# First samples of a speech joint kernel loaded in two halves, with its first products by halves of the channels

## The chip, the cores and the metric

The kernel runs on one core of a Trainium2 chip, alone. A core has TensorE (PE in the profile; its weight loads are listed as PEld), VectorE (DVE), ScalarE (ACT), GpSimd (POOL) and SyncE (SP), which here issues nearly all transfers between the chip's DRAM and the core's memory SBUF. TensorE writes its products into PSUM, eight banks of 512 columns of fp32; VectorE and ScalarE take them from there. The metric is the device time of one execution in microseconds, and the time of a kernel is the median of its runs.

## The reference

Two convolutions of five taps with a stride of two, a projection, and an outer sum over eight label positions with a tanh and a last product. `gelu` is the tanh approximation.

```python
B, T, D, K, U = 2, 4000, 512, 5, 8
h = gelu(sum(xp[:, i:i+T, :] @ w1[i] for i in range(K)))[:, ::2, :]
f = gelu(sum(hp[:, i:i+T1, :] @ w2[i] for i in range(K)))[:, ::2, :]
fe, ge = f @ w_f, g @ w_g
j = tanh(fe[:, :, None, :] + ge[:, None, :, :])
return j @ w_o            # (2, 1000, 8, 512), bf16
```

`xp` and `hp` are padded by two zeros on both sides. The taps of the first convolution are called tap 0 to tap 4 below.

## The kernel before

All operations are first collected as a list (`Plan.op`, `Plan.dma`) with what they read and write; the list's index is the operation's number. `ORDER` then holds, written out as steps from one number to the next, the order in which each engine runs them; SP's queue of transfers is one of these orders. `Plan.edges` finds the dependences, `Plan.emit` puts a semaphore wait ahead of each operation that needs one, and `AFTER` adds a few waits by hand. The costs that operations carry (`cost`, `rate`, `slack`) belong to a model that orders the closing waits; they don't change an instruction. An engine runs its queue strictly in order, so an operation that waits holds up all behind it.

Most of both convolutions is done with a transform: for three outputs at once, sums and differences of samples (`row`, `xa`, `xp`) are multiplied with sums and differences of weights (`w1_t`, `w1_x`), which VectorE and ScalarE make from the taps (`w1part`, helpers at L442, L604 and L605). Until these weights exist, the first 378 outputs of the first sequence are made directly from the taps (`direct`, L762). That is the head of the kernel, and the change is there:

- `load_xr(0)` (L494) brings 512 samples, four consecutive rows to a partition, into `xr[0]` with one transfer of 512 KB; `load_xr(1)` brings 256 more after the first has landed. The taps follow in the order 0, 4, 2, 1, 3 (`TAPS`), 512 KB each, with the transposing loads of `xa` (`load_a`) between them. A few of these issues wait for an earlier landing (`came`).
- Eight warming products of 512 columns on constants (`NWARM`, L550) keep TensorE at work until the samples are there.
- `turn(pp, cost)` (L563) transposes the samples with products against a unit matrix, so that channels lie on the partitions: pp 0 for even output columns (taps 0, 2, 4), pp 1 for odd ones (taps 1, 3). It is called once for each. A call takes both pairs of rows of all four channel blocks; pp 0 is evicted to `eo` in three pieces (one of 512 columns by VectorE, two of 256 by ScalarE), pp 1 in one piece of 1024 by ScalarE. `turn_more` (L585) does the same for `xr[1]`, with two evictions.
- `direct(i, lo, hi)` runs, for each of four blocks of outputs m, four products (the four channel blocks k) of tap i on the columns lo to hi, and adds them up in PSUM bank m. Taps 0, 4 and 2 run first on 254 columns (`NH`), those that the first 512 samples feed, with `turn_more` before tap 2; then these three taps run on the other 124 columns; taps 1 and 3 run on all 378.

After the last tap ScalarE applies gelu from the four banks, and TensorE goes on with the transformed products: first "t2" of the object `xa`, which needs the difference that the step "t2" of `Triple.step` makes in `xa` on VectorE, and the weights `w1_x[1]`.

Much later, `ge` (L807) computes `g @ w_g` and copies its 64 columns to `geT` on ScalarE in `NG` = 24 pieces. From about the middle on (`Seven`, L1063) the last product is computed in groups of seven products for eight, with sums `ss` made by GpSimd or VectorE, evictions `sn` and `og`, and stores to DRAM.

Of the kernel before, what the change touches and what calls it, by code (L numbers as in the profile page):

```python
# [61 lines left out]
        4 1 1 25 4 25 1 1 4 25 4 25 1 1 4 25 4 25 1 1 4 25 4 23 1 1 4 23 4 19 1 1 7 3 3 5 5""",  # L62
}
AFTER = """
    779:726 780:748 854:893 1059:1031 1178:1120 1272:1211 1273:1304 1364:1397 1456:1426 1486:1517 1603:1577"""


class View:
# [1234 lines left out]
```

## Time and profile before

| | us |
|---|---|
| median of 3 runs | 249.22 |
| lowest, highest | 248.97, 250.26 |
| the profiled execution | 248.89 |
| its span, first to last instruction | 247.6 |

The span is what the profile sees; the execution took 1.3 us more. A row of the timeline gives start, length, engine, line, operation, output<-input and count, and in brackets the idle time ahead of it with what ended it. A row of groups gives count, busy time, mean nanoseconds of one, and the idle time ahead. A row of the windows gives a stretch, its length, then busy time with count for PE, PEld, DVE, ACT and POOL, then the granted clock, the share of the DMA engines and GB/s. SPq is SP issuing a transfer, not the transfer.

### The profile page before, as it was taken

To read this page: it belongs to the slowest core of one execution; us is meant where nothing else is said; L and a number is where in the kernel's file an instruction comes from. 1 tells how busy PE (TensorE), PEld (TensorE's weight loads), DVE (VectorE), ACT (ScalarE), POOL (GpSimd) and SP (SyncE) were. 2 spreads that over 40 slices of the span, in tenths; PEclk is the share of its full clock that TensorE was granted. 3 is DMA by queue.
4 is the path that set the end of the run, shared out by engine and by line. 5 is a ranking of instruction groups with operands and counts; after the bars stand their busy time and mean duration, and the time that the engine had idled before them with its cause. 6 is when DMAs were issued, how large, how long until landed. Compare 5 with 4: busy or idle time off the path is not lost.

```text
span 247.6 us, 5295 instructions
## 1 busy us (share of the span) xinstructions
PE 244.1 (99%) x1966; PEld 184.5 (75%) x1968; DVE 212.4 (86%) x391; ACT 196.7 (79%) x355; POOL 88.0 (36%) x97
## 2 busy tenths in 40 slices
PE   8999999999999999999999999999999999999995
PEld 4969976666666666666456888777888888888884
DVE  1799996967999994795959988889999998899984
ACT  4897848458786475645599999799999999999863
POOL 1000000000000000000003988958988677658770
PEclk9999999999999999999999999999999999999999
DMA  7999999989000061000001044232543464653468
GB/s 236 303 217 186 158 189 182 195 183 345 6 3 0 0 213 45 0 3 1 0 3 42 10 134 143 76 111 85 173 129 101 156 192 149 226 180 106 161 217 283
DMA packets 54839, 31.83 MB, mean 129 GB/s; under 512 B 31870, under 2 KB 54558, under 8 KB 54814
## 3 DMA queue, kind: packets, MB, share of 16 engines
q1 hardware_dynamic: 54526, 31.34, 47.5%
q8 instruction: 15, 0.25, 0.5%
q10 hardware_dynamic: 288, 0.16, 0.2%
q14 instruction: 10, 0.08, 0.1%
HBM read 7.60 MB, written 16.38 MB: 97 GB/s over the span
## 4 chain that ended last, share of the span: by engine, by line
PE 98%; ACT 0%; issue 0%
PE acc L455 98%; PE acc L571 0%; ACT jT L447 0%; PE acc L592 0%; ACT ost L447 0%
## 5 line engine op out<-in xcount | busy, mean ns | idle before, releaser
L447 ACT ACTIVATE jT<-feT,geT 128x1000 bf16<-128x1000 f32 (+4 forms) x72 | 73.3, 1067 | 1.6 <-POOL ss L1085 1.3
L442 DVE TENSOR_TENSOR og<-acc,sn 128x512 bf16<-128x512 f32 x90 | 58.0, 684 | 2.5 <-PE acc L455 1.3
L1085 POOL TENSOR_TENSOR ss<-jT 128x512 f16<-128x512 bf16 x38 | 43.7, 1159 | 39.8 <-ACT jT L447 35.0
L455 PE MATMUL acc<-tw,ss 128*128 128x256 f16 x360 | 50.3, 273 | 0.0
L455 PE MATMUL acc<-row,jT 128*128 128x334 bf16 (+2 forms) x288 | 49.9, 296 | 0.0
L455 PE MATMUL acc<-wo_sb,jT 128*128 128x256 bf16 (+3 forms) x266 | 40.7, 277 | 0.1
L455 PEld LDWEIGHTS acc<-tw,ss 128*128 128x128 f16 x360 | 34.3, 98 | 6.8 <-ACT sn L556 1.0
L455 PEld LDWEIGHTS acc<-row,jT 128*128 128x128 bf16 x288 | 27.2, 97 | 11.3 <-DVE acc L598 0.7
L556 ACT ACTIVATE sn<-acc 128x512 f32<-128x512 f32 x55 | 32.4, 624 | 3.3 <-PE acc L455 3.2
L455 PEld LDWEIGHTS acc<-wo_sb,jT 128*128 128x128 bf16 x268 | 25.9, 98 | 5.7
L447 ACT ACTIVATE hT<-acc 128x334 bf16<-128x334 f32 (+3 forms) x36 | 15.2, 431 | 16.3 <-PE acc L455 16.2
L447 ACT ACTIVATE sd<-acc 128x334 f32<-128x334 f32 (+2 forms) x48 | 20.4, 434 | 8.9 <-PE acc L455 7.7
L557 DVE COPY sn<-acc 128x512 f32<-128x512 f32 x35 | 23.6, 686 | 3.3 <-PE acc L455 3.1
L455 PE MATMUL acc<-xp,jT 128*128 128x334 bf16 (+1 forms) x144 | 26.4, 305 | 0.0
L1085 POOL TENSOR_TENSOR ss<-ss,jT 128x512 f16<-128x512 f16 x19 | 22.0, 1159 | 9.9 <-DVE ss L1085 7.6
L1085 POOL TENSOR_TENSOR ss<-jT,ss 128x512 f16<-128x512 bf16 x19 | 22.0, 1160 | 6.8 <-DVE ss L1085 6.6
L439 POOL MEMSET hT<- 128x8 bf16 (+2 forms) x6 | 0.8, 148 | 56.0 <-ACT hT L447 43.7
L442 DVE TENSOR_TENSOR row<-row 128x1336 bf16<-128x1336 bf16 (+2 forms) x24 | 19.2, 813 | 0.0
L455 PEld LDWEIGHTS acc<-xp,jT 128*128 128x128 bf16 x144 | 14.0, 97 | 6.4
L455 PE MATMUL acc<-wo_sb,ss 128*128 128x256 bf16 x120 | 18.5, 273 | 0.0
L598 DVE SCALAR_TENSOR_TENSOR acc<-acc,sd 128x334 f32<-128x334 f32 (+2 forms) x24 | 11.8, 494 | 7.6 <-PE acc L455 7.4
L455 PE MATMUL acc<-tw,jT 128*128 128x256 f16 x120 | 18.0, 273 | 0.0
(113 smaller groups left out, 395.0 us busy)
## 6 DMA issues: line engine op xcount, KB each, us to landing
out_dram<-og SPq DMA_DIRECT2D x44, 256.0 KB
jT<-in_w_dram SPq DMA_DIRECT2D x10, 512.0 KB, 6.0
out_dram<-og SPq DMA_DIRECT2D x16, 128.0 KB, 2.0
xr<-in_x_dram SPq DMA_DIRECT2D x1, 512.0 KB, 3.4
wf_sb<-in_w_f_dram SPq DMA_DIRECT2D x1, 512.0 KB, 3.8
wg_sb<-in_w_g_dram SPq DMA_DIRECT2D x1, 512.0 KB, 4.8
wo_sb<-in_w_o_dram SPq DMA_DIRECT2D x1, 512.0 KB, 7.0
out_dram<-ost SPq DMA_DIRECT2D x4, 128.0 KB, 1.9
```

What stands on the lines that cost most here:

```text
L439: pl.op("pool", lambda e: e.memset(v.ap, 0.0), (), (v,))
L442: pl.op(eng, lambda e: e.tensor_tensor(out=o.ap, in0=a.ap, in1=b.ap, op=op), (a, b), (o,), 0.02 + 2.14e-3 * o.ap.free_size() if eng == "po ...
L447: pl.op("act", lambda e: e.activation(o.ap, i.ap, func, scale=scale, bias=0.0 if bias is None else bias.ap), rd, (o,), o.ap.free_size() * ...
L455: ins = e.matmul(o.ap, lhsT=l.ap, rhs=r.ap, start=start and n == 0, stop=stop and n == len(pairs) - 1, skip_group_check=not check)
L556: pl.flex({"act": (lambda e: e.activation(o.ap, v.ap, ACT.Copy), 0.05 + n * 0.833e-3), "dve": (lambda e: e.tensor_copy(out=o.ap, in_=v.ap) ...
L557: "dve": (lambda e: e.tensor_copy(out=o.ap, in_=v.ap), 0.065 + n * 1.04e-3)}, (v,), (o,))
L598: pl.op(eng, lambda e: e.scalar_tensor_tensor(out=o.ap, in0=a.ap, scalar=f, in1=b.ap, op0=ALU.mult, op1=add), (a, b), (o,), vec_cost(o, (a ...
L1085: fn = lambda e, o=S[i], x=x, y=y, op=op: e.tensor_tensor(out=o.ap, in0=x.ap, in1=y.ap, op=op)
```

## The change

In the head:

- `xr[0]` comes in two transfers of 256 KB, `load_x2(0)` with the first two rows of each partition and `load_x2(1)` with the other two. The second samples (`load_xr(1)`) wait for the second of these.
- Taps 0 and 4 come in two transfers each, channel blocks 0 and 1, then 2 and 3 (`load_w1h`). The queue is: samples, samples, tap 0, tap 0, first half of tap 4, second samples, second half of tap 4, tap 2, and then as before.
- The transposes of the first rows (both pp) are two operations that wait for the first half of the samples alone; those of the second rows follow by channel block for pp 0 and in two pieces for pp 1. Each channel block of pp 0 lies in a PSUM bank of its own (`KB`) and is evicted by itself: blocks 0 and 1 by VectorE, 2 and 3 by ScalarE, 256 columns each.
- `direct` takes a slice of channel blocks. Tap 0 and tap 4 run on 254 columns in two halves of the channels each, with `turn_more` between the halves of tap 4; then both on the other 124 columns; tap 2 runs once, on 378 columns.
- Six warming products in place of eight.

Elsewhere: `NG` is 28; the modelled rate and size of the stores are other numbers. The orders of all engines are written anew. In the head, both evictions of `turn_more` go to ScalarE; VectorE gives up two scalings of `w_x` and one of `row` and gets four scalings of 512 columns; one difference of `xp` (index 220 before) comes later on VectorE. Up to about 185 us the order of TensorE is otherwise the same but for a few exchanges; behind it the orders of TensorE, VectorE and ScalarE differ in many places, with the same operations. Some entries of `AFTER` are others.

```diff
-    NWARM = 8
+    NWARM = 6
...
-    NG = 24
+    NG = 28
...
-        came = [load_xr(0)]
+        def load_x2(half):
+            dst = xr[0][2 * half:2 * half + 2].map(lambda a: a.rearrange("p r k c -> p r (k c)"))
+            src = x[0, 0:4 * P, :].rearrange("(p r) c -> p r c", r=4)[:, 2 * half:2 * half + 2]
+            return pl.dma("sp", lambda e: e.dma_start(dst.ap, src), (), (dst,), nbytes=2 * P * 1024, rate=370e3, slack=0.1 * half)
+
+        load_x2(0)
+        came = [load_x2(1)]
...
-        came.append(load_w1(TAPS[0]))
-        came.append(load_w1(TAPS[1]))
-        came.append(load_xr(1, came[0]))
+        def load_w1h(i, *ks):
+            for k in ks:
+                v, src = w1_sb[i, k:k + 2], w1[i].rearrange("(k c) d -> c k d", c=P)[:, k:k + 2]
+                o = pl.dma("sp", lambda e, v=v, src=src: e.dma_start(v.ap, src), (), (v,), nbytes=262144, slack=(0.5 if i == TAPS[1] else 0.2) if k else 0.2)
+            return o
+
+        came.append(load_w1h(TAPS[0], 0, 2))
+        load_w1h(TAPS[1], 0)
+        load_xr(1, came[0])
+        came.append(load_w1h(TAPS[1], 2))
         came.append(load_w1(TAPS[2], came[0]))
         load_a(4, 0, after=came[1])
-        came.append(load_w1(TAPS[3], came[-3]))
+        came.append(load_w1(TAPS[3], came[-2]))
         load_a(2)
-        came.append(load_w1(TAPS[4], came[-3]))
+        came.append(load_w1(TAPS[4], came[-2]))
         load_a(1, 3, 5)
...
+        KB = (4, 1, 5, 6)
+
+        def turned(pp, k):
+            if pp:
+                at_k = psb[:, 7 * 1024:8 * 1024].rearrange("p (k r c) -> p r k c", r=2, k=NK)[:, :, k]
+                return View(at_k, np.array([7]), True)
+            at_k = psb[:, KB[k] * 1024:KB[k] * 1024 + 2 * P].rearrange("p (r c) -> p r c", r=2)
+            return View(at_k, np.array([KB[k]]), True)
+
+        def turn(pp, r, ks, cost):
+            v = [turned(pp, k) for k in ks]
+
+            def fn(e):
+                for k, pv in zip(ks, v):
+                    ins = e.transpose(pv.ap[:, r], xr[0].h[:, 2 * r + pp, k, :], ident.h[:, :])
+                return ins
+            pl.op("pe", fn, (xr[0][2 * r + pp], ident[:]), tuple(v), cost * len(ks))
+
+        def turn_out(pp, k=None):
+            if pp:
+                v = View(psb[:, 7 * 1024:8 * 1024].rearrange("p (k r c) -> p k c r", r=2, k=NK), np.array([7]), True)
+                o = eo[1, :, 16:16 + 2 * P].map(lambda a: a.rearrange("p k (c r) -> p k c r", r=2))
+                act(o, v, ACT.Copy)
+                return
+            o = eo[0, k, 16:16 + 2 * P].map(lambda a: a.rearrange("p (c r) -> p c r", r=2))
+            v = turned(0, k).map(lambda a: a.rearrange("p r c -> p c r"))
+            if k < 2:
+                pl.op("dve", lambda e, o=o, v=v: e.tensor_copy(out=o.ap, in_=v.ap), (v,), (o,), vec_cost(o, (v,)))
+            else:
+                act(o, v, ACT.Copy)
...
-        def direct(i, lo=0, hi=ND):
+        def direct(i, lo=0, hi=ND, ks=slice(0, NK)):
             for m in range(NK):
                 mm(ps.cols(m * NT + lo, hi - lo),
-                   [(w1_sb[i, k, m * P:(m + 1) * P], eo[i % 2, k, 15 + i // 2 + lo:15 + i // 2 + hi]) for k in range(NK)],
-                   i == TAPS[0] and lo == 0, i == TAPS[-1], False)
+                   [(w1_sb[i, k, m * P:(m + 1) * P], eo[i % 2, k, 15 + i // 2 + lo:15 + i // 2 + hi]) for k in range(NK)[ks]],
+                   i == TAPS[0] and lo == 0 and ks.start == 0, i == TAPS[-1], False)
...
-        turn(0, 0.215)
-        direct(TAPS[0], 0, NH)
-        turn(1, 0.215)
-        direct(TAPS[1], 0, NH)
-        turn_more(0.46)
-        direct(TAPS[2], 0, NH)
-        for i in TAPS[:3]:
+        turn(0, 0, range(NK), 0.095)
+        turn(1, 0, range(NK), 0.095)
+        for k in range(NK):
+            turn(0, 1, (k,), 0.095)
+            turn_out(0, k)
+        for k in range(0, NK, 2):
+            turn(1, 1, range(k, k + 2), 0.095)
+        turn_out(1)
+        for i in TAPS[:2]:
+            for k in range(0, NK, 2):
+                direct(i, 0, NH, slice(k, k + 2))
+                if i and not k:
+                    turn_more(0.46)
+        for i in TAPS[:2]:
             direct(i, NH, ND)
+        direct(TAPS[2])
         for i in TAPS[3:]:
             direct(i)
```

The first numbers of the orders of VectorE and of SP, the rest of which is as long as the kernel's list (SP: 6 and 7 the samples, 9 and 10 tap 0, 11 and 13 tap 4, 12 the second samples, 14 tap 2):

```diff
     "dve": """
-        0 46 50 1 2 -4 3 3 3 -41 44 13 -12 1 33 -26 9 -8 27 -1 -32 7 16 -29 -3 34 9 -18 26 -6 -25 -9 8 27 -36 18 20 -1 2
+        0 49 2 55 6 -7 3 -1 13 9 -11 9 -8 6 26 -47 9 3 36 -9 -2 -31 1 23 2 -22 40 -17 8 -23 8 -9 35 -17 18 1 2 -1 2 3
...
     "sp": """
-        6 2 1 1 1 1 1 1 1 1 1 1 1 2 2 1 1 1 1 2 1 1 1 1 1 248 1 1 1 1 1 1 2 1 1 1 1 1 254 1 1 168 3 33 33 4 1 1 30 4 33
+        6 1 2 1 1 1 1 1 1 1 1 1 1 1 1 1 2 2 1 1 1 1 2 1 1 1 1 1 254 1 1 1 1 1 1 2 1 1 1 1 1 254 1 1 172 3 33 33 4 1 1 30
```

More of the change, by code (lines that the diff above doesn't have):

```diff
@@ L561, in evict @@
                 pl.op("dve", lambda e: e.tensor_copy(out=o.ap, in_=v.ap), (v,), (o,), vec_cost(o, (v,)))
-        def turn(pp, cost):
-            for bk, k0, k1 in (((4, 0, 2), (5, 2, 3), (6, 3, 4)), ((7, 0, 2), (7, 2, 4)))[pp]:
-                at_k = psb[:, bk * 1024:(bk + 1) * 1024].rearrange("p (k r c) -> p r k c", r=2, k=NK)[:, :, k0:k1]
-                pv = View(at_k, np.array([bk]), True)
-                def fn(e, pv=pv, k0=k0, k1=k1):
-                    for k in range(k0, k1):
-                        for r in range(2):
-                            ins = e.transpose(pv.ap[:, r, k - k0, :], xr[0].h[:, 2 * r + pp, k, :], ident.h[:, :])
-                    return ins
-                pl.op("pe", fn, (xr[0][:], ident[:]), (pv,), cost * (k1 - k0))
-                if pp:
-                    if k0 == 0:
-                        continue
-                    k0, pv = 0, View(psb[:, bk * 1024:(bk + 1) * 1024].rearrange("p (k r c) -> p r k c", r=2, k=NK), pv.cells, True)
-                o = eo[pp, k0:k1, 16:16 + 2 * P].map(lambda a: a.rearrange("p k (c r) -> p k c r", r=2))
-                v = pv.map(lambda a: a.rearrange("p r k c -> p k c r"))
-                if k0 or pp:
-                    act(o, v, ACT.Copy)
-                else:
-                    pl.op("dve", lambda e, o=o, v=v: e.tensor_copy(out=o.ap, in_=v.ap), (v,), (o,), vec_cost(o, (v,)))
@@ L1020, in store2 @@
             dst = out[b, t:t + 2 * P, u, :].rearrange("(t p) d -> p t d", p=P)
-            pl.dma("sp", lambda e: e.dma_start(dst, s.ap), (s,), (), sem_of(key), 4 * P * P * 4)
+            pl.dma("sp", lambda e: e.dma_start(dst, s.ap), (s,), (), sem_of(key), 4 * P * P * 4, 350e3)
         def store(jt, src, key, eng="sp", cl=slice(0, NT)):
@@ L1030, in store @@
                 dst = out[b, t:t + n, u, cl]
-                pl.dma(eng, lambda e, s=s, dst=dst: e.dma_start(dst, s.ap), (s,), (), sem_of(key), 2 * n * P * 4)
+                pl.dma(eng, lambda e, s=s, dst=dst: e.dma_start(dst, s.ap), (s,), (), sem_of(key), 2 * n * (cl.stop - cl.start), 350e3)
                 lo += n
```

16 lines of the change are left out of this document (8 added, 8 removed), and 59 rows, old and new, of the table ORDER.

## The prediction

> **What bounds the kernel now.** I read the page first (busy shares), then the chain that ended last, then the first 20 us as a timeline.
>
> ```profile
> span 247.6 us, 5295 instructions
> PE 244.1 (99%) x1966; PEld 184.5 (75%) x1968; DVE 212.4 (86%) x391; ACT 196.7 (79%) x355; POOL 88.0 (36%) x97
> ...
> 0.77 3.57 PE acc L455 x8
> ...
> 5.04 0.67 ACT jT L447 x2
> ...
> 5.79 3.66 PE acc L455 x32
> 9.45 0.45 PE acc L592 x8
> 9.90 120.64 PE acc L455 x928
> ```
>
> TensorE is the bound: the chain stays on it from 9.90 us to the end. A change of the head can only pay by letting products start earlier, and each microsecond must then survive 235 us of stages whose other queues are nearly full. What holds the head:
>
> ```profile
> 0.74 0.39 SPq L482 DMA_DIRECT2D xr<-in_x_dram  x1
> 1.19 0.97 SPq L473 DMA_DIRECT2D jT<-in_w_dram  x2
> 4.15 0.34 SPq L482 DMA_DIRECT2D xr<-in_x_dram  x1
> 4.17 1.31 PEld L571 LDWEIGHTS acc<-ident,xr 128*128 128x128 bf16 x16 [0.73 <-DMA xr<-in_x_dram]
> 4.83 0.69 DVE L583 COPY jT<-acc 128x512 bf16<-128x512 bf16 x1 [3.70 <-PE acc L571]
> 5.04 1.69 ACT L447 ACTIVATE jT<-acc 128x256 bf16<-128x256 bf16 x3 [2.81 <-PE acc L571]
> 5.76 3.41 PEld L455 LDWEIGHTS acc<-jT 128*128 128x128 bf16 x32 [0.28 <-ACT jT L447]
> 7.50 0.43 DVE L442 TENSOR_TENSOR hw<-jT 128x512 f16<-128x512 bf16 x1 [1.98 <-DMA jT<-in_w_dram]
> 16.79 0.27 PEld L455 LDWEIGHTS acc<-jT 128*128 128x128 bf16 x3 [0.29 <-DMA jT<-in_w_dram]
> ```
>
> The samples land at 4.15, the transposes run from 4.18, the evictions to SBUF end at 5.7, the first product starts at 5.79. The last two rows matter as much: VectorE starts its weight sums only when the whole of tap 4 is there (7.50), and at 16.79 the last tap's products already wait for their weights.
>
> **The first product.** Prices of TensorE come from the groups by form of the first 20 us, those of DMA from the issues (size, time to landing):
>
> ```profile
> L455 PE MATMUL acc<-const-bfloat16-1.0 128*128 128x512 bf16 x8 | 3.6, 628 | 0.8 <-PEq L1288 0.8
> L571 PE MATMUL acc<-ident,xr 128*128 128x128 bf16 x16 | 1.5, 268 | 0.0
> L455 PE MATMUL acc<-jT 128*128 128x254 bf16 x48 | 5.6, 272 | 0.1
> L455 PE MATMUL acc<-jT 128*128 128x124 bf16 x48 | 2.8, 217 | 0.0
> L455 PE MATMUL acc<-jT 128*128 128x378 bf16 x32 | 5.4, 323 | 0.0
> ...
> xr<-in_x_dram SPq DMA_DIRECT2D x1, 512.0 KB, 3.4
> out_dram<-ost SPq DMA_DIRECT2D x4, 128.0 KB, 1.9
> xr<-in_x_dram SPq DMA_DIRECT2D x1, 256.0 KB, 4.0
> ```
>
> A half load of the samples (256 KB) is not in the trace with an empty queue. Its bounds are 1.9 us (128 KB) and 3.4 us (512 KB); on the line between them it takes 2.4, so it lands between 2.6 and 4.15. I take 3.4, nearer the larger load, because that one is also the first of the kernel. The second half lands when the whole load did, 4.15 to 4.25. Six warming products end at 0.77 + 6 x 0.45 = 3.4, so the removed two cost nothing there. The eight transposes of the first half (0.1 each at the early, slow pace) run 3.45 to 4.3. From 4.3 the four of the even rows follow, one for each channel block; each is evicted by itself. The eviction of 512 columns took 0.69 on VectorE; 256 columns are half of that, 0.35, two in sequence: from 4.66 (the copy began 0.65 after the first transpose now, 0.35 after one alone) to 5.37. With the 0.09 of issue, the first product starts at 5.45 instead of 5.79: a gain of **0.34**, between 0 (the second half lands late, or VectorE's two copies cost 0.5 each) and 0.45 (transposes at 4.18). Its two blocks of tap 0 are there: the whole of tap 0 had landed before 5.79.
>
> **The products behind it.** Their number on 254 columns stays at 32 for taps 0 and 4; by halves of channels the same instructions come in another order. Tap 2 becomes 16 products of 378 columns (5.4 / 32 x 16 = 2.70) instead of 16 of 254 (1.87) and 16 of 124 (0.93): 0.1 less by busy sums, which hold the overlap at each group's end; I take 0.02 and keep 0 to 0.1. The eight transposes L592 move between the halves of tap 4. Tap 4's second half is now issued behind the wait for the second samples and behind the later samples (xr, 256 KB). That is the place in the stream where these landed: 4.15 + 4.0 = 8.15. TensorE reaches it at 5.45 + 24 x 0.109 + 0.45 = 8.5 (step 3.66 / 32 less the drain). No stall, 0.35 to spare. SP now has five issues instead of three ahead of its first wait (about 0.45 each, to 3.1, below 4.2), and behind it three instead of two; the transposing load after them waited until 5.56 for tap 0 anyway, so the order behind is late by nothing. The uncovered price would be 0.45.
>
> **The last tap.** TensorE would reach it 0.36 earlier, at 16.4, but it waited for the weights until 16.79. That load was issued at 10.54:
>
> ```profile
> jT<-in_w_dram SPq DMA_DIRECT2D x1, 512.0 KB, 6.2
> ...
> 15.40:16.40 1.00, 1.00 (x8) 0.58 (x6) 1.00 (x4) 0.94 (x2) 0.00 (x0) 1.00 0.28 29
> ...
> q8 instruction: 1, 0.02, 5.8%
> ```
>
> The last two columns of the second row are DMA share and GB/s: from 15.4 to 16.4 us almost nothing moves, as when one engine is behind the others. The third row is from 13.2 to 14.4: a fetch of instructions went through one engine there. I take it for TensorE's code, which would be fetched as TensorE proceeds through it (not shown by this row); 18 pairs of instructions fewer come before it then, so it moves to about 14.2, when most of the tap is through. I estimate the landing at 16.4, between 15.5 (fetch out of the way) and 16.75 (as now). So of 0.36 some 0.35 would pass here, or only the present stall if nothing changes.
>
> **VectorE's queue.** This is what caps the gain:
>
> ```profile
> 7.50:37.20 29.70, 29.70 (x301) 25.20 (x300) 29.26 (x67) 23.26 (x50) 0.77 (x6) 1.00 1.10 203
> ...
> L557 DVE COPY jT<-acc 128x512 bf16<-128x512 bf16 x1 | 0.4, 426 | 0.0
> L605 DVE TENSOR_SCALAR row<-xa 128x832 bf16<-128x832 bf16 x2 | 0.8, 376 | 0.0
> L605 DVE TENSOR_SCALAR w_x<-hw 128x512 bf16<-128x512 f16 x2 | 0.6, 291 | 0.0
> ...
> 18.37 0.59 DVE L442 TENSOR_TENSOR xa<-xa 128x824 bf16<-128x824 bf16 x1
> 19.37 0.25 PE L455 MATMUL acc<-xa,w_x 128*128 128x206 bf16 x1
> ```
>
> VectorE (fourth pair of figures) is busy 29.26 of 29.70 us from the landing of tap 4 on. With tap 4 whole only at 8.15 it starts 0.65 later. The order text takes from it one eviction (0.43), two scalings of w_x (0.29 each) and one of row (0.38), and gives it four scalings of 512 columns (0.29 each, nearest row): 0.23 less. About 0.2 more were waits for ScalarE near 10 us, which vanish. So the difference that the first product on xa needs ends at 18.96 + 0.65 - 0.43 = 19.18 instead of 18.96, and that product starts at 19.2 instead of 19.37. ScalarE takes 1.4 us more but has 6.4 us free in that window (29.70 - 23.26).
>
> The sum of the head: 0.36 earlier, cut to **0.2** by VectorE; 0 to 0.4 with the bounds above.
>
> **The rest.** Four more copies of geT (24 to 28) cost ScalarE 0.07 each, 0.28, by the first row below; ScalarE waits 2.41 behind them (second row), which hides it, and uncovered it costs 0.28. From about 185 us on the order of all engines is another one; the work is the same. What it can win is what TensorE waits for there:
>
> ```profile
> 115.26 1.55 ACT L447 ACTIVATE geT<-acc 128x3 f32<-128x3 f32 x22
> 119.70 0.45 ACT L447 ACTIVATE fT<-acc 128x334 bf16<-128x334 f32 x1 [2.41 <-PE acc L455]
> ...
> PEld acc L455 <- ACT sn L556: 1.3, 7, 0.3
> PEld acc L455 <- DVE og L442: 0.4, 2, 0.3
> ```
>
> These are load-side waits of 1.7 us in all; part is hidden under running products. A reshuffle may win or lose about 0.4 of it. I take 0.
>
> The profiled execution took 248.89 us (span 247.6 and 1.3 around it); the sum gives 248.7 for its like. The median of the runs, 249.22, is 0.33 above that execution, so I predict 249.0.
>
> **The clock.** By the first group above a warming product costs 3.6 / 8 = 0.45 us for 512 columns, 0.88 ns a column; 378 columns later take 0.45 ns a column. The fast pace begins among the transposes:
>
> ```profile
> 4.18:4.99 0.81, 0.81 (x8) 0.81 (x9) 1.00 1.06 374
> 5.11:5.60 0.49, 0.49 (x9) 0.38 (x7) 1.00 1.02 324
> ```
>
> Eight in 0.81 us, then nine in 0.49: the pace doubles near 5.1, 4.3 us after the first product. If it doubles there again, nothing is lost. The Trainium skill ("TensorE: Matmul & The Clock Gate", Part 1) says that the clock opens after a busy window of about 3.4 us that runs freely; the trace's 4.3 us does not contradict it. The same page's Part 4 says that transposes don't count as busy; by that rule this change, which puts transposes and a gap of 0.3 us where two warming products were, could miss the window. No run here shows which.
>
> **Rivals.**
> (a) *The clock opens one window later* (slower). Of the 3.4 us before 5.1 now 2.5 are products; with six warming products 1.7. If that decides, the pace doubles at 5.1 + 3.4 = 8.5, and products from 5.45 to 8.5 run at half pace: 3.05 / 2 = 1.5 us lost, less the 0.36 gained: 1.1 slower, **250.3**. For it: fewer products before the turn. Against: the transposes keep the array busy, and the pace turned while they ran. Decides from a start of fast products after 6 us on.
> (b) *VectorE's later start comes through* (slower). If the moved work doesn't shrink its queue, 0.65 late less 0.41 (the time between 18.96 and 19.37) is 0.25, and the later reader at 30.80 us sees up to 0.4 of it: **249.6**. For: the 29.26 of 29.70. Against: 0.43 of relief counted above.
> (c) *All of the head and a better tail*: 0.36 + 0.4: **248.45**. For: the last tap may land at 15.5, ahead of its readers. Against: VectorE.
> (d) *The split does not split*: both halves land near 4.15, the first transposes start there, and the even rows' only at 5.0; the first product is at 6.1, 0.3 late: **249.5**. Against: the loads stand in one queue in order; the Trainium skill ("DMA: Bandwidth & Descriptors", Queues, rings and completion order) has each DMA engine take its descriptors in ring order, which no run here shows yet.
>
> **Chances.** Forecast 0.50, (a) 0.12, (b) 0.18, (c) 0.15, (d) 0.05. The forecast's own range is 248.6 to 249.4, the sum's 0 to 0.4 and 0.2 for the median of few runs. A difference under 0.5% (1.25 us: 247.97 to 250.47) cannot be told from no change by a measurement of this kernel, whose three runs spread from 248.97 to 250.26. A third of (c) goes below it: 0.05. Of (a) half goes above, and a little of (b) and (d): 0.09. The rest, 0.86, is no change. The range, 248.2 to 250.2, reaches over (b), (d), most of (c) and to the edge of (a).
>
> **What would show it.** First transpose near 3.45, first product near 5.45, VectorE's first sum near 8.2, the last tap's first product before 16.6 without a wait, the first product on xa at 19.2. The forecast is wrong if the pace doubles after 6 us, if that last product is not before 19.37, or if TensorE's waits after 185 us differ by more than 0.4.

## The result and the profile after

| | before | after |
|---|---|---|
| median of 11 runs each | 249.19 (248.73 to 250.26) | 250.44 (249.87 to 250.73) |
| the profiled execution | 248.89 | 250.59 |
| its span | 247.6 | 249.2 |
| first product on xa | 19.37 | 21.42 |

The ratio is 1.0049, with a 95% interval of 1.0037 to 1.0061: slower by half a per cent, 1.25 us. The loss is in the head: the first product on xa is 2.05 us late, and the execution ends 1.70 late. First the page of the changed kernel, its span, its busy line and the chain that ended last by engine:

```profile
span 249.2 us, 5278 instructions
...
PE 245.1 (98%) x1948; PEld 184.9 (74%) x1950; DVE 211.3 (85%) x390; ACT 197.6 (79%) x361; POOL 87.9 (35%) x97
...
PE 97%; DMA 2%; DVE 0%; issue 0%; SPq 0%; ACT 0%
```

TensorE is still the bound, and it is busy 1.0 us more than before with 18 recorded products fewer (two warming ones, and 16 by tap 2 in one piece). Its timeline in the head shows where:

```profile
3.39 1.03 PE L591 MATMUL acc<-ident,xr 128*128 128x128 bf16 x8
5.09 1.03 PE L591 MATMUL acc<-ident,xr 128*128 128x128 bf16 x8 [0.66 <-DMA xr<-in_x_dram]
6.22 4.37 PE L456 MATMUL acc<-jT 128*128 128x254 bf16 x24
10.43 0.61 PE L615 MATMUL acc<-ident,xr 128*128 128x128 bf16 x8
10.88 10.52 PE L456 MATMUL acc<-jT 128*128 128x254 bf16 x88
21.42 0.80 PE L456 MATMUL acc<-xa,w_x 128*128 128x206 bf16 x7
```

The first transposes start at 3.39 as forecast. The second ones wait for the second half of the samples until 5.09, the first product runs at 6.22 and not at 5.45, and 24 products take 4.37 us where 32 took 3.66 before. The windows tell why: in two microseconds of products on 254 columns TensorE (first pair of figures) does 10 in the changed kernel and did 19 in the kernel before.

```profile
6.30:8.30 2.00, 2.00 (x10) 1.40 (x11) 0.00 (x0) 0.90 (x1) 0.00 (x0) 1.00 0.96 286
```

```profile
5.85:7.85 2.00, 2.00 (x19) 1.72 (x20) 0.35 (x2) 1.23 (x2) 0.00 (x0) 1.00 1.07 369
```

The clock column says 1.00 in both, so the pace has to be read from the products. By their starts in the trace, the step halves to 0.109 us at 9.5 in this execution; before, it did so among the transposes at 5.1. From 10.88 to xa TensorE shows no wait (gaps under 0.15 us are not listed); VectorE's difference, which the first product on xa needs too, ends at 21.36 (shown under VectorE further down).

Second, the loads. SP's timeline after:

```profile
0.74 0.87 SPq L498 DMA_DIRECT2D xr<-in_x_dram  x2
1.65 1.46 SPq L521 DMA_DIRECT2D jT<-in_w_dram  x3
5.06 0.34 SPq L483 DMA_DIRECT2D xr<-in_x_dram  x1
5.44 0.45 SPq L521 DMA_DIRECT2D jT<-in_w_dram  x1
5.93 0.47 SPq L474 DMA_DIRECT2D jT<-in_w_dram  x1
6.50 3.77 SPq L493 DMA_TRANSPOSE xa<-in_x_dram  x2
10.32 0.58 SPq L474 DMA_DIRECT2D jT<-in_w_dram  x1
```

The same rows before, from tap 2 on:

```profile
4.53 0.44 SPq L473 DMA_DIRECT2D jT<-in_w_dram  x1
5.56 3.03 SPq L492 DMA_TRANSPOSE xa<-in_x_dram  x2
8.64 0.58 SPq L473 DMA_DIRECT2D jT<-in_w_dram  x1
```

Tap 2 is issued 1.40 late (5.93), the transposing loads 0.94 (6.50), tap 1 1.68 (10.32). Completions, from the semaphore records of the traces ("again" is a second trace of the changed kernel, e18 below; us from the start of the span):

```
                      before   after   again
samples, last part      4.13    5.04    4.71
tap 0, last part        5.55    6.49    6.17
tap 4, last part        7.47    8.58    8.61
tap 2                   9.57   11.07   10.60
tap 1                  13.24   14.59   16.13
tap 3                  16.75   18.14   18.39
```

The windows of 2 us, first before, then after (the last two columns are the DMA share and GB/s):

```profile
2.00:4.00 2.00, 2.00 (x6) 0.61 (x4) 0.00 (x0) 0.22 (x2) 0.00 (x0) 1.00 0.91 322
...
6.00:8.00 2.00, 2.00 (x21) 1.71 (x19) 0.51 (x2) 1.23 (x2) 0.00 (x0) 1.00 1.07 368
```

```profile
2.00:4.00 2.00, 2.00 (x10) 0.92 (x9) 0.00 (x0) 0.22 (x2) 0.00 (x0) 1.00 0.83 255
...
6.00:8.00 2.00, 1.90 (x11) 1.28 (x10) 0.17 (x1) 1.20 (x3) 0.00 (x0) 1.00 1.01 285
```

At 2 to 4 us 67 GB/s are missing and at 6 to 8 us 83: (67 + 83) x 2 us = 300 KB less moved, about a microsecond of DMA. So two things were late, the pace and the loads. Which of them costs the time?

### The profile page after: what moved, and what is told of

Its sections match the earlier page's. It is cut to its first block, busy times and chain, and to the rows that moved or that the text cites. A ratio compares the mean times of both kernels' runs of the same rounds, so it can differ in the third digit from the quotient of the medians.

```text
span 249.2 us, 5278 instructions
## 1 busy us (share of the span) xinstructions
PE 245.1 (98%) x1948; PEld 184.9 (74%) x1950; DVE 211.3 (85%) x390; ACT 197.6 (79%) x361; POOL 87.9 (35%) x97
## 4 chain that ended last, share of the span: by engine, by line
PE 97%; DMA 2%; DVE 0%; issue 0%; SPq 0%; ACT 0%
PE acc L456 96%; DMA xr<-in_x_dram 2%; DVE jT L604 0%; PE acc L615 0%; SPq L498 0%; PE acc L591 0%; ACT ost L448 0%
## 5 line engine op out<-in xcount | busy, mean ns | idle before, releaser
L456 PE MATMUL acc<-tw,ss 128*128 128x256 f16 x360 | 49.1, 273 | 0.0
L456 PE MATMUL acc<-wo_sb,jT 128*128 128x256 bf16 (+3 forms) x266 | 41.7, 277 | 0.1
L570 ACT ACTIVATE sn<-acc 128x512 f32<-128x512 f32 x57 | 34.1, 636 | 3.9 <-PE acc L456 3.6
L448 ACT ACTIVATE hT<-acc 128x334 bf16<-128x334 f32 (+3 forms) x36 | 15.1, 430 | 16.2 <-PE acc L456 16.0
L571 DVE COPY sn<-acc 128x512 f32<-128x512 f32 x33 | 22.4, 685 | 2.9 <-PE acc L456 2.7
L621 DVE SCALAR_TENSOR_TENSOR acc<-acc,sd 128x334 f32<-128x334 f32 (+2 forms) x24 | 11.8, 491 | 7.2 <-PE acc L456 7.0
```

The source lines that it names most:

```text
L448: pl.op("act", lambda e: e.activation(o.ap, i.ap, func, scale=scale, bias=0.0 if bias is None else bias.ap), rd, (o,), o.ap.free_size() * ...
L456: ins = e.matmul(o.ap, lhsT=l.ap, rhs=r.ap, start=start and n == 0, stop=stop and n == len(pairs) - 1, skip_group_check=not check)
L570: pl.flex({"act": (lambda e: e.activation(o.ap, v.ap, ACT.Copy), 0.05 + n * 0.833e-3), "dve": (lambda e: e.tensor_copy(out=o.ap, in_=v.ap) ...
L571: "dve": (lambda e: e.tensor_copy(out=o.ap, in_=v.ap), 0.065 + n * 1.04e-3)}, (v,), (o,))
L621: pl.op(eng, lambda e: e.scalar_tensor_tensor(out=o.ap, in0=a.ap, scalar=f, in1=b.ap, op0=ALU.mult, op1=add), (a, b), (o,), vec_cost(o, (a ...
```

## The experiments

All were timed in five rounds against the kernel before. That kernel's median differs from batch to batch (249.05 to 250.06 in the five), so only ratios within a batch are compared. The theories: **C**, the late clock; **D**, the loads are late; within D **Q**, the queue runs dry around SP's waits, and **S**, split loads cost more by themselves; **P**, the new order of products; **F**, a fetch of instructions holds up a load; **L**, VectorE's late start; **T**, both C and D, each enough alone. First the table to which the paragraphs refer. "Full pace" is when the step of products or transposes halves, "tap 1" its completion, both from the trace's records; xa is its first product.

| run | warming | full pace | tap 1 | xa | profiled us | ratio and interval |
|---|---|---|---|---|---|---|
| before | 8 | 5.1 | 13.24 | 19.37 | 248.89 | |
| after | 6 | 9.5 | 14.59 | 21.42 | 250.59 | 1.0049 [1.0037, 1.0061] |
| e1 | 8 | 4.7 | 15.56 | 21.01 | 250.16 | 1.0054 [1.0037, 1.0071] |
| e2 (before, six) | 6 | 5.0 | 13.61 | 19.77 | 249.00 | 1.0004 [0.9988, 1.0019] |
| e3 | 6 | by 4.2 | 15.64 | 21.09 | 250.19 | 1.0044 [1.0029, 1.0059] |
| e4 | 6 | by 5.8 | 14.82 | 20.27 | 249.41 | 1.0033 [1.0018, 1.0048] |
| e5 | 6 | by 4.8, lost 7.7 to 11.2 | 15.08 | 23.15 | 252.29 | 1.0105 [1.0070, 1.0139] |
| e6 | 6 | by 4.2 | 13.66 | 19.82 | 248.91 | 0.9979 [0.9956, 1.0002] |
| e7 | 8 | by 3.9 | 14.99 | 20.44 | 249.60 | 1.0013 [0.9989, 1.0037] |
| e8 | 6 | by 4.3 | 14.75 | 20.19 | 249.28 | 1.0018 [0.9996, 1.0040] |
| e9 | 6 | 9.7 | 11.67 | 21.50 | 250.61 | 1.0015 [0.9991, 1.0038] |
| e10 (before, small ones) | 5 | 7.0 | 13.74 | 20.16 | 251.59 | 1.0052 [1.0023, 1.0080] |
| e11 | 6 | 9.8 | 11.37 | 21.44 | 250.53 | 0.9998 [0.9974, 1.0022] |
| e12 | 6 | 9.7 | 11.84 | 21.45 | 250.64 | 1.0065 [1.0042, 1.0088] |
| e13 | 8 | 5.0 | 13.21 | 22.58 | 251.82 | 1.0074 [1.0045, 1.0104] |
| e14 | 8 | by 4.2 | 11.86 | 21.09 | 250.25 | 1.0005 [0.9980, 1.0030] |
| e15 | 8 | by 4.5 | 11.36 | 20.52 | 249.66 | 0.9992 [0.9972, 1.0013] |
| e16 (before, three) | 3 | 7.2 | 12.75 | 20.05 | 249.30 | 1.0031 [1.0005, 1.0056] |
| e17 | 8 | by 4.1 | 13.48 | 19.89 | 249.02 | 0.9965 [0.9943, 0.9988] |
| e18 (after again) | 6 | by 4.8 | 16.13 | 21.58 | 250.76 | 1.0031 [1.0005, 1.0058] |

**One part at a time: e1 to e4.** e1 gives the changed kernel eight warming products, e2 gives the kernel before six.

```diff
-                mm(ps.cols(0, NT), [(z, zz)], True, True)
+                mm(ps.cols(0, NT), [(z, zz)] * (3 if i + 1 == n else 1), True, True)
```

> The changed kernel with eight warming products in place of six (its last warming operation issues three); nothing else differs. Theory C (clock): the changed kernel's loss comes from products at half pace, because TensorE pauses between the two groups of transposes and its fast pace begins one window later (9.4 us in its profile). Theory D (transfers): it comes from the second half of the samples, which landed at 5.04 instead of 4.15 us, and from SP's queue, which waited for it. C expects the pause to close (warming to 4.2, transposes to 5.0, then the second half), the fast pace before 6.3, and 249.0 to 249.5. D expects 250.2 to 250.6, first product at 6.2 as in the changed kernel, second tap's issue still at 5.9.

> The kernel before with six warming products in place of eight, nothing else. TensorE then pauses from 3.4 to 4.15 us. C expects the fast pace to begin later in many executions and 249.7 to 250.3. D expects 249.1 to 249.3, no difference.

In e1 the pace doubled at 4.7, and nothing was gained:

```profile
5.94 2.80 PE L456 MATMUL acc<-jT 128*128 128x254 bf16 x24 [0.46 <-DVE jT L604]
...
15.70 5.32 PE L456 MATMUL acc<-jT 128*128 128x378 bf16 x32 [1.19 <-DMA jT<-in_w_dram]
21.01 1.24 PE L456 MATMUL acc<-xa,w_x 128*128 128x206 bf16 x12
```

The 24 products took 2.80 instead of 4.37 us, but then TensorE waited 1.19 us for a tap's weights, and xa came at 21.01, only 0.41 earlier. e2 costs nothing either. So the clock is not the cause by itself. e3 brings the first samples in one load again, e4 takes away SP's wait for them ahead of the second samples and tap 2:

```diff
-        load_x2(0)
-        came = [load_x2(1)]
+        came = [load_xr(0)]
```

```diff
-        load_xr(1, came[0])
+        load_xr(1)
...
-        came.append(load_w1(TAPS[2], came[0]))
+        came.append(load_w1(TAPS[2]))
```

> The changed kernel with the first samples in one load of 512 KB again (landing 4.15 by the profile before), the rest of the change kept, six warming products. The transposes then run 4.2 to 5.9 or less without a pause, the first product starts near 6.0, the later transfers are issued when they were before. D expects 249.2 to 249.6. C expects TensorE's pause to be only moved (3.4 to 4.15) and 249.9 to 250.4.

> The changed kernel without the wait of SP for the second half of the samples (the second samples and tap 2 are issued at once). D in its queue part expects the issues behind it at about 3.5 to 5.6 us instead of 5.06 to 6.5, the last tap's weights landed by 16.8 instead of 18.1, and 249.5 to 250.0. C expects no gain over 0.2 (250.2 to 250.6), since TensorE is behind by its half pace anyway.

e3 keeps the loss, with tap 1 at 15.64 although the samples came whole at 4.13: with whole samples, split taps still go with a late tap 1. e4 wins back 1.2 us in its profile and a third of the loss in its ratio, where the intervals still overlap.

**Loads together: e5 to e8.** e5 has whole taps and split samples, e6 whole samples and whole taps (the loads of before in their old order), e7 is e4 with eight warming products, e8 is e4 with one sample load.

```diff
-        came.append(load_w1h(TAPS[0], 0, 2))
-        load_w1h(TAPS[1], 0)
+        came.append(load_w1(TAPS[0]))
+        came.append(load_w1(TAPS[1]))
         load_xr(1, came[0])
-        came.append(load_w1h(TAPS[1], 2))
```

> The changed kernel with taps 0 and 4 each in one load again; the samples stay split in two loads, the products by halves, their order and the six warming products stay. Theory Q (the DMA queue runs dry, because SP's wait for the samples now has only 768 KB ahead of it and each issue behind it needs some 2 us to its first packet): with both whole taps ahead of the wait the gap at 6 to 8 us closes, only the one later issue of tap 0 (0.45 us) remains, 249.3 to 249.6, VectorE's first sum at 7.9 to 8.3, the first product on xa at 19.5 to 19.9. Theory S (256 KB tap loads cost more by themselves): 249.2 to 249.6 too, so this run does not tell Q from S. Theory P (the new order of the products or VectorE's sums): 250.2 or more. Theory C (the clock alone): 250.2 or more, unless the clock opens before 5.5.

> The changed kernel with the samples in one load and taps 0 and 4 in one load each, so that the loads are those of the kernel before in their old order; products by halves, their order, the second samples between and six warming products stay. Theory Q: nothing of the loss is left, 248.6 to 249.1, landings within 0.2 of the kernel before (last tap 16.8), first product on xa 19.2 to 19.5. Theory S: the same. Theory P: 250.2, with landings as before but VectorE late. Theory C: 249 to 250.2, by where the clock opens.

> The changed kernel, without SP's wait ahead of the second samples and tap 2, and with eight warming products. If wait (Q) and clock (C) each hold it up, the two edits together do more than either alone (250.16 and 250.45): 249.2 to 249.6, full pace at 4.8 and the first product on xa at 19.5 to 19.9. If only Q counts: 249.9 to 250.2, as without the wait alone. Theory S: 250 or more.

> The changed kernel with the first samples in one load and without SP's wait ahead of the second samples and tap 2; taps 0 and 4 stay split by channels. Theory Q: tap 0 issued as early as in the kernel before and no dry queue at 6 to 8 us, 248.8 to 249.2, last tap landing at 16.5 to 17. Theory S (the 256 KB loads cost more whatever the order): 249.8 or more. Theory P: 250.2.

e6 settles the largest question: with the old loads, and products by halves, new orders and six warming products all kept, nothing is lost. P falls. From e3 it differs in the split of taps 0 and 4 alone (ratio 1.0044 there, 0.9979 here; tap 1 at 15.64 and 13.66), so that split is enough for the loss. e5 went against Q and S alike, the slowest of all. Its tap 0, one load behind two, completed at 7.99, TensorE stood still for 2.6 us, and the granted clock (0.50 in the window below the timeline's row) fell to half:

```profile
8.08 4.25 PE L456 MATMUL acc<-jT 128*128 128x254 bf16 x24 [2.63 <-issue]
```

```profile
7.80:11.00 3.20, 2.92 (x15) 2.07 (x16) 1.49 (x5) 0.00 (x0) 0.00 (x0) 0.50 1.16 261
```

Why a whole tap behind split samples takes so long stays open. e7 and e8 win back most of the loss by their ratios, but not all that Q promised: tap 1 still completes at 14.75 to 14.99 though it was issued at 9.1 to 9.5, so something else holds it.

**The fetch: e9 to e12.** In the records of transfers, one packet of 16 KB of instructions goes through one of the 16 DMA engines in the head. Beside it stand the slowest packet of 256 bytes of the next transposing load and tap 1 (us):

```
            before   e2     e6    e17   after    e1    e3    e4    e7    e8   e18
fetch        13.30 13.69  13.77  13.73  14.70 12.32 12.22 12.87 13.03 12.82 12.56
it took       1.10  1.13   1.09   0.94   1.05  0.93  1.01  0.95  0.95  0.90  1.64
slow packet   1.27  1.24   1.24   1.27   1.30  1.60  1.10  1.64  1.37  1.72  2.37
tap 1        13.24 13.61  13.66  13.48  14.59 15.56 15.64 14.82 14.99 14.75 16.13
```

In each, a transposing load then waits about as long as the fetch took or longer. In the five on the left the fetch starts just behind tap 1's completion, in the six on the right ahead of it, and there tap 1 is late: from issue to completion it took 4.27 to 4.89 us on the left and 5.04 to 6.27 on the right. Two things are against reading too much into it. In e5, which is not in the table, tap 1 is late (15.08) with the fetch far behind it (17.45). And slow packets come without a fetch too: in e13, below, such packets take up to 1.79 us from 11.2 on, and 15 to 80 GB/s move from 12.2 to 12.9, with the fetch only at 14.18. To test F, e9, e11 and e12 issue tap 1 ahead of xa's transposing loads, in e8, in e6 and in the changed kernel; e10 lengthens TensorE's program in the kernel before, so that the fetch should come earlier.

```diff
-        load_a(4, 0, after=came[1])
-        came.append(load_w1(TAPS[3], came[-2]))
+        came.append(load_w1(TAPS[3]))
+        load_a(4, 0, after=came[1])
```

```diff
-                mm(ps.cols(0, NT), [(z, zz)], True, True)
+                if i < 5:
+                    mm(ps.cols(0, NT), [(z, zz)], True, True)
+                else:
+                    z8 = zz.map(lambda a: a[:, 0:8])
+                    mm(ps.cols(0, 8), [(z, z8)] * (20 if i == 5 else 1), True, True)
```

> The run with one sample load, split taps and no wait of SP ahead of the second samples (249.28 in its profile, tap 1 complete at 14.75), with one edit more: tap 1's load is issued right behind tap 2's, ahead of the two transposing loads of xa. Theory F (a 16 KB instruction fetch, at 12.82 there, makes one of 16 DMA engines 0.9 us late, the transposing load behind tap 1 then holds the other 15, and tap 1's completion comes only behind it): tap 1 completes before the fetch, at 10.5 to 12, TensorE has no wait of 0.67 ahead of its 378-column products, first product on xa at 19.2 to 19.7, total 0.5 to 1.0 lower than that run, 248.7 to 249.3 beside 249.2 of before. Theory L (VectorE's late start at 8.5 is what remains): first product on xa stays at 20.0 to 20.3, total unchanged. A loss is possible too: xa's phases come 1.5 us later and VectorE may wait for them at 12.

> The kernel before, with its last three warming products replaced by 22 small ones of 8 columns (the other five stay), so that TensorE's program is 19 products longer ahead of the first sample product and nothing else differs. Theory F: the instruction fetch comes when TensorE is at about the same place of its program, so 1 to 2 us earlier than 13.30, at 11.3 to 12.5; it then makes an engine late while tap 1 is on its way, tap 1 completes at 14.2 to 14.8 instead of 13.24, first product on xa at 19.6 to 20.2 instead of 19.37, total 249.3 to 249.9. If fetches do not matter: tap 1 at 13.2 to 13.5, total within 0.3 of before. If the small products hold the transposes up (past 4.2), the run does not tell.

> The run with the loads of the kernel before (one sample load, whole taps; products by halves and six warming products stay; 249.09), with tap 1's load issued ahead of xa's transposing loads. Theory F: tap 1 completes at 10.5 to 11.5 and no later fetch can hold it; the 378-column products start at 11.9 as there and run through, the last tap is then next: 248.6 to 249.2, first product on xa at 19.2 to 19.8. Theory L: the same total as there, since VectorE's chain from 7.9 sets xa.

> The changed kernel with one edit: tap 1's load is issued right behind tap 2's, ahead of xa's two transposing loads (and without its wait for tap 4). If the 2 us of the change come mostly from tap 1's late landing at 14.59 behind the transposing loads (Q and F): tap 1 at 11.5 to 12.5, first product on xa at 20.2 to 20.8 instead of 21.42, total 249.3 to 249.9. If they come from tap 2's late landing (11.07) and VectorE's late start (8.60) alone: first product on xa at 21.0 to 21.5, total 250.2 to 250.6.

Tap 1 now completed at 11.4 to 11.8 in three kernels, and xa came at 21.44 to 21.50 in all three, as in the changed kernel. Their profiled executions share one thing, a pace that doubles at 9.7 to 9.8. TensorE of e11:

```profile
6.01 4.60 PE L456 MATMUL acc<-jT 128*128 128x254 bf16 x24
10.45 0.61 PE L613 MATMUL acc<-ident,xr 128*128 128x128 bf16 x8
10.90 10.53 PE L456 MATMUL acc<-jT 128*128 128x254 bf16 x88
21.44 0.80 PE L456 MATMUL acc<-xa,w_x 128*128 128x206 bf16 x7
```

From 10.90 it is the changed kernel's row to 0.02 us, with other loads. So with the late clock xa comes at 21.4 to 21.5 under four different sets of loads, and that gave theory T. VectorE's difference on xa ends there at 21.36 to 21.44, again just ahead of xa: it had waited 0.73 to 1.94 us for ScalarE, which stood behind the late transposes of `turn_more`. The late pace thus reaches xa by two ways. e10 did not move this fetch forward (13.66, though its program has 19 more products ahead), so it does not test F. Its profiled execution lost the last 1.6 us at the final stores, with another fetch among them (246.00), so its time is no price either.

**Both causes: e13 to e18.** e13 to e15 are e12, e9 and e11 with eight warming products (the edit of e1). e16 is the kernel before with three full warming products, the other five on 8 columns, e17 is e6 with eight, e18 the changed kernel as it is.

```diff
-                mm(ps.cols(0, NT), [(z, zz)], True, True)
+                w = NT if i < 3 else 8
+                mm(ps.cols(0, w), [(z, zz.map(lambda a: a[:, 0:w]))], True, True)
```

> The changed kernel with two edits together: eight warming products, and tap 1's load ahead of xa's transposing loads. Theory T (two causes, a late clock and late taps, each of which alone puts the first product on xa at 21.0 to 21.5): full pace by 5, tap 1 complete by 13.5 to 14, first product on xa at 19.8 to 20.4, ratio to before 0.999 to 1.002, where each edit alone gave 1.0054 and 1.0065. A third cause (products by halves, VectorE's order): first product on xa stays above 21 and the ratio stays at 1.004 or more. If the clock opens late in the profiled run in spite of eight products: 21.4 again.

> As the run before it, with the samples in one load and without SP's wait ahead of the second samples. Theory T: as there or 0.2 to 0.4 lower, full pace by 4.5, tap 1 by 11 to 12, first product on xa at 19.3 to 20.0, ratio 0.996 to 1.000. A third cause: ratio 1.002 or more, which the same kernel with six warming products gave (1.0015, full pace only from 9.75).

> One sample load, whole taps, tap 1's load ahead of xa's, products by halves, eight warming products. Theory T: nothing is late, full pace by 5, tap 1 by 11.5, the last tap or VectorE sets the first product on xa at 19.2 to 19.9; 248.6 to 249.0 where the kernel before has 249.1, ratio 0.996 to 0.999. Without the two extra products it gave 0.9998 and in its profile full pace only from 9.80 and 250.53.

> The kernel before with the last five of its eight warming products cut to 8 columns, so that TensorE is idle from about 2.3 to 4.2; nothing else differs. If the clock opens only behind enough steady work (theory C's mechanism): full pace not before 7 and probably at 8 to 10, the 378-column products and the first product on xa later, at 20.5 to 21.4, total 249.9 to 250.8 with loads as in the kernel before (tap 1 at 13.2 to 13.7). If the clock does not depend on it: full pace at 4 to 5, xa 19.4, total as before.

> One sample load, whole taps in the order of the kernel before, eight warming products; of the change only the products by halves, the orders of the engines and the tail stay. Theory T: both causes are away, full pace by 5.1, first product on xa at 19.3 to 19.8, 248.5 to 249.0 where before has 249.0 in the same state, ratio 0.995 to 0.999. A third cause in the products by halves or in VectorE's order: ratio above 1.001.

> The changed kernel itself, for a second trace. Theory T: either full pace from 9 to 10 and the first product on xa at 21.4 to 21.5, or full pace by 6, tap 1 complete only at 14.5 to 15.6 and the first product on xa at 20.0 to 21.1; ratio 1.003 to 1.007 in both. If full pace comes by 6 and xa still comes at 21.4, TensorE's pace was not what set it in the first trace.

e13 missed: the pace doubled at 5.0 and tap 1 was there at 13.21, but tap 3 only at 18.42 and xa's phases later still, and TensorE waited for both:

```profile
18.46 2.73 PE L456 MATMUL acc<-jT 128*128 128x378 bf16 x16 [1.26 <-DMA jT<-in_w_dram]
22.58 1.24 PE L456 MATMUL acc<-xa,w_x 128*128 128x206 bf16 x12 [1.38 <-DVE xa L443]
```

Moving tap 1 forward only passed the delay to the loads behind it; TensorE of e14 and e15 waits 1.39 and 0.99 us for VectorE in the same way. It is no repair. e16 prices the clock with old loads: the pace doubles at 7.2, the 32 products take 4.35 instead of 3.66 us, and xa comes 0.68 later, less than expected.

```profile
5.86 4.35 PE L455 MATMUL acc<-jT 128*128 128x254 bf16 x32
...
20.05 1.15 PE L455 MATMUL acc<-xa,w_x 128*128 128x206 bf16 x11
```

e18 shows that the loss does not need the late clock. This execution of the same kernel had the full pace by 4.8 (19 products in 2 us again), and was no faster. Its chain of waits, a window of its early products, and the timelines of TensorE and VectorE behind them:

```profile
2.12 4.04 DMA jT<-in_w_dram
...
6.18 1.34 SPq L493
...
7.57 2.24 SPq L493
...
9.86 6.28 DMA jT<-in_w_dram
...
16.27 13.74 PE acc L456 x125
```

```profile
5.90:7.90 2.00, 2.00 (x19) 1.78 (x20) 0.00 (x0) 0.81 (x1) 0.00 (x0) 1.00 0.99 300
```

```profile
16.27 5.32 PE L456 MATMUL acc<-jT 128*128 128x378 bf16 x32 [1.98 <-DMA jT<-in_w_dram]
21.58 0.62 PE L456 MATMUL acc<-xa,w_x 128*128 128x206 bf16 x5
```

```profile
16.16 0.29 DVE L628 TENSOR_SCALAR jT<-jT 128x512 bf16<-128x512 bf16 x1 [1.35 <-DMA jT<-in_w_dram]
...
20.93 0.59 DVE L443 TENSOR_TENSOR xa<-xa 128x824 bf16<-128x824 bf16 x1
```

The chain runs from tap 0's second half through SP's transposing loads, which wait for it, into tap 1, for which TensorE idles 1.98 us and VectorE 1.35; then come 5.32 us of products, VectorE's work up to 21.52, and xa. The expectation says of such an outcome that TensorE's pace did not set xa in the first trace; how much it can have cost there is estimated under rival (a) below. The transfers from 12.4 to 16.2 us, DMA share in tenths and GB/s in 40 slices:

```profile
DMA  9999999999999989990000000000000000000499
GB/s 377 550 356 356 366 377 356 337 345 334 340 305 248 224 197 186 156 46 11 11 0 11 11 11 11 11 11 22 22 32 22 22 22 22 19 16 19 97 275 291
...
q8 instruction: 1, 0.02, 2.7%
```

The fetch is in this stretch (q8), and some 1.8 us follow (19 slices of 0.095) in which no more than 32 GB/s move; the last packets of 1 KB there come one at a time, until 15.59. The kernel before has such a hole too, but at 15.4 to 16.4 (a row of the prediction), when tap 1 had long arrived; there it held tap 3, at 16.75.

## Why the prediction was wrong

The forecast was 249.0, between 248.2 and 250.2; 250.44 was measured. Point by point:

- **The first half of the samples** at 3.4 held: 3.35, with transposes at 3.39. **The second half** "when the whole load did, 4.15 to 4.25" did not: 5.04 and, again, 4.71. With it fell the first product, 5.45 in the forecast, 6.22 and 5.83 in the traces, later than the 5.79 of before. "Its two blocks of tap 0 are there" failed too: the first half of tap 0 completed at 5.80 and 5.42, so 5.45 could not be had in the first trace, and only just in the second.
- **The step that failed** is in the products behind it: "SP now has five issues instead of three ahead of its first wait ...; the transposing load after them waited until 5.56 for tap 0 anyway, so the order behind is late by nothing." SP's wait ends with the second half of the samples, 0.91 later; and tap 0, issued 0.46 later (1.65 instead of 1.19), completes at 6.49, so the wait of the transposing loads moves too. Behind these SP issues tap 1 at 10.32 instead of 8.64. The "uncovered price" of 0.45 was 1.35 us at tap 1 in one trace and 2.89 in the other. In the first, the later issue is all of it: from issue to completion tap 1 took 4.27 us, no more than the 4.60 of before. In the second, 1.22 is the later issue and 1.67 a longer way (6.27), with the fetch ahead of it. e6 and e17, with the old loads, show the whole loss gone.
- **The last tap** was to land at 16.4, the fetch of instructions having moved "to about 14.2, when most of the tap is through". It landed at 18.14 and 18.39. The fetch came at 14.70, or, at full pace, at 12.56, ahead of tap 1. That it counts TensorE's instructions was my assumption, and e10 speaks against it.
- **Rival (a), the late clock**, had 0.12 and 250.3. In the first trace it came: half pace from 6.22 to 9.5 is (9.5 - 6.22) / 2 = 1.6 us, and with the first product's 0.43 that is the 2.05. But full pace would not have given 1.6 back. Tap 3 landed at 18.14, and its 16 products take 2.7 (e13's row), so by this estimate xa could not come before 20.8; the clock adds 0.6 at most to what these loads cost. The second trace has the early clock and the same time, by the loads. So it was luck that the rival's number is near the median, and the late clock and the late loads do not add up: whichever ends last counts. Nor do the medians show a price of six warming products: the seven pairs on record that differ in six or eight alone (before and e2, after and e1, e4 and e7, e6 and e17, e9 and e14, e11 and e15, e12 and e13) have ratios that change with eight by -0.0020 to +0.0009, and in no pair do the intervals part.
- How often the clock is late with six warming products is not settled by one trace per kernel: of the eleven such traces four (after, e9, e11, e12) are late, at 9.5 to 9.8; of the seven with eight products none is, all by 5.1. The Trainium skill ("TensorE: Matmul & The Clock Gate", Part 1) says that the window of activity runs freely, so that the same kernel turns at different moments; the two traces of the changed kernel, at 9.5 and by 4.8, agree, but lie further apart than the half microsecond either way that the page gives.
- **VectorE**, taken for the cap, was one, later than the sum had it. In all sixteen traces with the changed orders its difference on xa ends 0.05 to 0.07 before the first product on xa; in the four of the kernel before it was ready 0.41 to 0.72 ahead. TensorE's own products end at most 0.2 earlier in thirteen of the sixteen, so the two arrive nearly together. The sum had 0.65 for a later start, 0.43 less work, and the waits for ScalarE gone. The rows of the first trace: a start 1.10 later (8.60 instead of 7.50), 1.06 of waiting for tap 2, 0.73 for ScalarE, and as the rest 0.49 less work: 18.96 + 1.10 + 1.06 + 0.73 - 0.49 = 21.36 instead of 19.18.

```profile
8.60 0.49 DVE L628 TENSOR_SCALAR hw<-jT 128x512 bf16<-128x512 bf16 x2 [2.44 <-DMA jT<-in_w_dram]
...
11.17 0.76 DVE L443 TENSOR_TENSOR jT<-hw,jT 128x512 bf16<-128x512 f16 x2 [1.06 <-DMA jT<-in_w_dram]
...
13.53 0.43 DVE L443 TENSOR_TENSOR hw<-hw,hw 128x512 f16<-128x512 f16 x1 [0.73 <-ACT hw L627]
...
20.77 0.59 DVE L443 TENSOR_TENSOR xa<-xa 128x824 bf16<-128x824 bf16 x1
```

```profile
10.86 0.60 ACT L570 ACTIVATE jT<-acc 128x512 bf16<-128x512 bf16 x1 [3.66 <-PE acc L615]
```

- **ScalarE** "has 6.4 us free", but not where it is needed: an eviction of `turn_more` now stands ahead of all its scalings, and it idles 3.66 us for those transposes (second fence), although tap 4 had landed at 8.58. With the old loads and the early clock (e17) VectorE still starts 0.50 later, waits 0.64 for tap 2 and 0.23 for ScalarE, and xa comes at 19.89 instead of 19.37. So the gain of the products by halves did not come even there. Rival (b) had the engine right, but not these waits. Of rival (d) the outcome came (second half at 5.0, first product at 6.2), not its mechanism: the halves did land apart.
- **The rest**, taken at 0 with 0.4 either way: from xa's first product to the end of the execution it took 229.52 us before, 229.17 and 229.18 after. But e2 and e16, which have the old order there, took 229.23 and 229.25. So with a later xa the old order takes up 0.3 as well, and the new one adds no more than 0.1.

What is left of the change is small. e17, the best version, is faster than the kernel before in its batch, 0.9965 [0.9943, 0.9988]; the lowest runs are alike (248.54 and 248.67), and it has none above 249.33, where the other has half above 250. What those runs of the kernel before wait for was not traced, and in the profiled executions e17 is not ahead (249.02 and 248.89).

## What to carry to other kernels

When a load is split, list again what each wait of the issuing queue has in flight ahead of it and which loads stand behind: the price falls on loads that the edit does not touch, here a tap that is needed at 14 us. When two late things run side by side, mending one can show nothing (the clock in e1, the loads in the trace of e11), and one trace names only the one that was last in that execution; take a second trace of the same kernel before the cause is named. Before a load or a transpose is moved, look at what stands behind its readers in the queues of the other engines: here ScalarE's scalings, and with them VectorE's sums, waited behind an eviction. And a version with all loads as they were (e6) tells more in one run than the single repairs did.

## What the runs showed of the hardware

A fetch of 16 KB of instructions occupies one of 16 DMA engines for 0.9 to 1.6 us in the table above, and packets of 256 bytes of the next transposing load then take up to 2.37 us. In e18 the load ahead of it, tap 1, moved its last packets one at a time until 15.59 and completed at 16.13. The Trainium skill ("Runtime: NRT & Kernel Launch", Instruction fetch mechanics) says that each engine's sequencer fetches its code in blocks of 16 KB over a DMA queue of its own, mostly hidden. The size agrees, 16384 bytes in the records; which engine a fetch is for no row tells, and the loads beside it were not spared. That the fetch causes the delay is read from eleven traces and not shown: no run moved it alone, and e13 has such a hole without one. One more case fits: in e10 a fetch at 246.00 falls among the final stores, which take 3.3 to 4.1 us to land where those of the kernel before take 2.0 to 2.3.

Full pace, once there, was lost again in a gap of 2.6 us without products (e5: 5.45 to 8.08, granted clock 0.50 from 7.8 to 11.0).
